# Block-masked attention with routed experts on one core: where the table scatters stand on GpSimd's queue

## The chip, the cores and the metric

The kernel runs on one core of a Trainium2 chip. A time is the device time of one execution in microseconds. The engines are TensorE (PE, with its weight loads as PEld), VectorE (DVE), ScalarE (ACT), GpSimd (POOL) and SyncE (SP, which issues DMAs). Each runs its own instructions in order and waits on semaphores for the others.

## The reference

Attention over 8 batches of 8 heads, 576 positions and 64 features, in which a position sees all blocks of 64 up to its own; then a layer of 8 experts of which each token uses one.

```python
mask = block_i >= block_j
scores = np.where(mask, scale * np.matmul(q, k.transpose(0, 1, 3, 2)), -1e9)
attn = np.exp(scores - np.max(scores, axis=-1, keepdims=True))
attn = attn / (np.sum(attn, axis=-1, keepdims=True) + 1e-09)
x = np.matmul(attn, v)               # then 4608 tokens of 512 features
expert_idx = np.argmax(logits, axis=1)
for e in range(E):                   # tokens grouped by expert
    mask = expert_idx == e
    h = np.maximum(x[mask] @ w1[e], 0.0)
    out[mask] = gate_w[mask, None] * (h @ w2[e])
```

## The kernel before, in words

The attention part (some 365 us) goes through 32 pairs of heads, four pairs to a batch. The expert part behind it takes the tokens in tiles of 128 that share an expert.

For a pair, `prep` turns q and k on TensorE (line 325); ScalarE and VectorE split them into a high and a low half (qh, ql, kh, kl, lines 342 and 344). `maxes` makes scores once to find each row's maximum (scores at line 360, maxima nmx on VectorE at 366); the maxima are turned and put beside q by a DMA (nmT, qa, lines 378 and 381). `scores` makes the scores again (line 421), ScalarE turns them into exponentials (pA and pT, line 428 and 430) and GpSimd adds these up over the key tiles into pS (`add`, lines 399, 400 and 402). `values` multiplies with v (line 456), and ScalarE copies the result out of PSUM as oe (line 462). `finish` turns oe and the sums back on TensorE, takes reciprocals (rin, line 531) and writes x into xrow. Scores live in four PSUM tiles (psm) that go round, so TensorE's next scores wait until ScalarE or VectorE has read the tile that it wants.

After a batch's fourth pair, `route` finds each token's expert and its place among that expert's tokens. It ends with five scatters (line 671): DMAs issued by GpSimd, each of which writes 128 token numbers of 4 bytes into places of `table` in DRAM. A scatter waits for nothing but an older DMA. At a batch's last scatter SyncE also issues one store of x (`store_piece`, line 575). Batch 5 (EB) is special: behind its scatters the first places of the table are read back (et, line 710), so that two tiles of tokens can be fetched early (line 716).

Each of these functions yields between its steps, and a string of letters per pair (`FIRST`, `STEADY`, `FINAL`) says which advances next: s for scores, v for values, m for maxes, p for prep, f for finish, l for loads, r for one step of the oldest unfinished route. That alone sets the order of instructions on every engine. STEADY has 11 letters r for pairs 5 to 26 (counted from 0); FINAL has a string for each of the last five.

Of the kernel before, what the change touches and what calls it, by code (L numbers as in the profile page):

```python
# [28 lines left out]
    "pfvvvvvpmvrvvrvpmrrssslmmsrsmrmmssprprsrvvsrvmfpfmfsrffm",  # L29
)  # L30
FINAL = (
    "rmmvrrvmvvvvrvvspvsrmpsrrrsrvfmvsvrrmrmfflsprrrfvvvrvmmrsfsffrrpvppsspvvppvmvssrrmrmvrvvmmrsmrsrmmsfrfsffssfprrrsmlvfprm",
    "srvmvpmmrvvrrvmrrrrvrrmppmmrrmvvrrrvvrrrrrmrrrrrrrlp",
    "slrvrrrrmrpsrprrsrsrspsrrrmmssrrrssrrrrrmssmmrmsrfrrfvvrvvrr",
    "rfvfsrrrmrrsmrfvfmrrrrsrrmsvmrvvrrvvrrsrrfrfrvfrrrsfvvfrsvvfvvrvrfrr",
# [13 lines left out]
def kernel(  # L49
# [522 lines left out]
    def store_piece():  # L572
        b, xrow, j = pieces.pop(0)
        r0 = b * S + 1 + j * P
        nc.sync.dma_start(xbuf[r0:r0 + P, :], xrow[:, j, :])
        if j == NJ - 2:
            nc.sync.dma_start(xbuf[r0 + P:r0 + P + 64, :], xrow[0:64, NJ - 1, :])
# [8 lines left out]
    def route(b, xrow, lgh, ssp):  # L586
# [80 lines left out]
            store(b, xrow, (NP - 1) * P, RW)  # L667
        yield
        if b < B - 1:
            for j in range(NJ):  # L670
                w = nc.gpsimd.indirect_dma_start(
                    out=table, out_offset=bass.IndirectOffsetOnAxis(ap=rowj[:, j:j + 1], axis=0),
                    in_=tokf[:, b, j:j + 1], in_offset=None, bounds_check=E * RE * P - 1, oob_is_err=False)
                for o in writes:
                    tc.declare_no_dep(w.ins, o.ins, reason="each place is written once")
                writes.append(w)
                if (b == B - 2 or j == NJ - 1) and pieces:
                    store_piece()
                yield
            if b == EB:  # L680
                early_g.append(early_rows())

    EB = B - 3
# [23 lines left out]
    def early_rows():  # L707
        et = rt.tile([P, EARLY], F32, name="et")
        none = rt.tile([P, EARLY], F32, name="enone")
        nc.sync.dma_start(et, table.rearrange("(p r) o -> p (r o)", p=P)[:, 0:EARLY])  # L710
        yield
        while pieces:
            store_piece()
        nc.gpsimd.tensor_copy(ei[:, 0], et)
        for u in range(EARLY):
            nc.gpsimd.indirect_dma_start(
                out=ex[u], out_offset=None, in_=xbuf[0:1 + (EB + 1) * S, :],
                in_offset=bass.IndirectOffsetOnAxis(ap=ei[:, 0, u:u + 1], axis=0))
            yield
        indices(nc.gpsimd, None, ei[:, 1], et, none)  # L720
# [63 lines left out]
    def post(n):  # L784

        b = n // NP
        xrow, rin, lgh, ssp = tiles(b)
        yield from finish(n, xrow, rin, lgh, ssp)
        if n % NP == NP - 1:
            slow.append(route(b, xrow, lgh, ssp))  # L790
        yield
# [400 lines left out]
    def chain():  # L1192
# [4 lines left out]
        for c in fg:  # L1197
            if c == "squares":
                break
            yield c  # L1200
        ch_sq.append(fg)
        rg = route(B - 1, xrow, lgh, ssp)
        for c in rg:
            if c == "counted":
# [106 lines left out]
    a, b = ea  # L1311
# [201 lines left out]
```

## Time and profile before

| | |
|---|---|
| median of 3 runs | 814.71 us (812.38 to 814.80) |
| profiled execution, its own time | 814.69 us |
| its span | 813.0 us |
| TensorE busy | 780.4 us (96%) |
| VectorE busy | 604.4 us (74%) |
| GpSimd busy | 436.4 us (54%) |
| ScalarE busy | 408.1 us (50%) |
| scatters of line 671 | 35, of 966 to 1157 ns (median 978) |

The span is the time from the first instruction to the last in the profiled execution; the execution's own time holds 1.7 us more. A busy share is a mean over stages with different limits. A timeline row gives the start (us from the span's start), the duration, the engine, the line, what is written and read, and in brackets the idle time ahead of it with what the profile thinks ended that. "issue" is a wait for which it found nothing.

### The profile page before, as it was taken

How to read it: one execution, taken by the hardware profiler on the slowest of the kernel's cores; microseconds unless marked ns; L12 is line 12 of the kernel's file. 1: busy time of each engine (PE TensorE's matmuls, PEld its weight loads, DVE VectorE, ACT ScalarE, POOL GpSimd, SP SyncE). 2: the span in 40 equal slices, each digit the busy share in tenths (PEclk: the TensorE clock that was granted, in tenths of full speed). 3: DMA queues.
4: the chain of work that ended last, by engine and by line, in shares of the span. 5: the costliest groups of instructions: out<-in, count | busy, mean ns of one | idle time of the engine just before them, and what ended most of it. 6: DMA issues, size and time to landing. Idle time of an engine off the chain costs nothing. (4 is left out here: it accounts for less than half of the span.)

```text
span 813.0 us, 23042 instructions
## 1 busy us (share of the span) xinstructions
PE 780.4 (96%) x7160; PEld 628.6 (77%) x7160; DVE 604.4 (74%) x1382; ACT 408.1 (50%) x831; POOL 436.4 (54%) x420
## 2 busy tenths in 40 slices
PE   8999999999989998889999999999999999999996
PEld 3688877787878776668778887788888888888885
DVE  6668777786868686659858777777887778877881
ACT  2566756575757564664745355553533332543222
POOL 7555767667666756772337278675661111561110
PEclk9999999999999999999999999999999999999999
DMA  4745364544444543163835347444441111111111
GB/s 104 167 104 138 82 163 99 152 104 122 104 126 100 139 100 100 29 241 118 293 129 179 106 157 225 160 158 158 144 146 54 54 55 42 40 49 54 54 36 39
DMA packets 141422, 93.96 MB, mean 116 GB/s; under 512 B 118925, under 2 KB 120541, under 8 KB 141260
## 3 DMA queue, kind: packets, MB, share of 16 engines
q1 hardware_dynamic: 133228, 69.74, 30.8%
q0 software_dynamic: 8032, 22.36, 8.4%
q8 instruction: 66, 1.08, 0.5%
q14 instruction: 96, 0.79, 0.3%
HBM read 72.71 MB, written 19.71 MB: 114 GB/s over the span
## 5 line engine op out<-in xcount | busy, mean ns | idle before, releaser
L1167 DVE STREAM_TRANSPOSE pt<-h 32x256 f32<-32x256 f32 x528 | 240.7, 456 | 31.2 <-ACT h L1141 14.0
L366 DVE TENSOR_REDUCE nmx<-psm 128x16 f32<-128x1024 f32 (+2 forms) x128 | 125.5, 985 | 22.0 <-PE psm L360 19.4
L912 POOL TENSOR_TENSOR ring_l<-raw,ring_h 128x1024 f32 (+1 forms) x49 | 116.2, 2400 | 37.5 <-ACT ring_h L907 23.8
L1181 POOL DMA_INDIRECT out_dram<-y,outi x36 | 37.2, 1034 | 177.5 <-ACTq L1061 118.1
L1114 PE MATMUL py<-ring_h,hh 128*128 x272 | 109.3, 402 | 0.8 <-ACT h L1141 0.8
L1114 PE MATMUL py<-ring_l,hh 128*128 x272 | 106.3, 391 | 0.0
L428 ACT ACTIVATE pT<-psm 128x640 f32<-128x640 f32 (+2 forms) x128 | 89.0, 702 | 27.2 <-PE psm L360 15.8
L402 POOL TENSOR_TENSOR pS<-pS,pT 128x640 f32<-128x640 f32 (+2 forms) x93 | 93.4, 1004 | 10.4 <-ACT pT L430 2.8
L1114 PE MATMUL py<-ring_h,hl 128*128 x272 | 88.8, 389 | 0.0
L1114 PE MATMUL ph<-ring_h,xh 128*128 x280 | 86.5, 390 | 1.7 <-ACT y L1180 1.1
L1114 PE MATMUL ph<-ring_l,xh 128*128 x280 | 86.4, 390 | 1.5 <-POOLq L1073 1.5
L456 PE MATMUL psm<-pT,vo 128*64 128x320 f32 (+2 forms) x640 | 76.1, 380 | 0.3 <-ACT pT L428 0.3
L1180 ACT ACTIVATE y<-py,xg 128x512 f32<-128x512 f32 x34 | 23.4, 688 | 103.2 <-PE py L1114 99.7
L1175 DVE TENSOR_TENSOR hl<-pt,hh 128x512 fp32r<-128x512 f32 x66 | 42.5, 686 | 42.6 <-ACT hh L1173 37.6
L421 PE MATMUL psm<-qh,kh 64*128 64x320 f32 (+4 forms) x384 | 66.9, 344 | 7.1 <-ACT pT L428 3.6
L907 ACT CAST ring_h<-raw 128x1024 f32 (+1 forms) x62 | 60.9, 1048 | 22.3 <-POOLq L1073 9.7
L1173 ACT CAST hh<-pt 128x512 fp32r<-128x512 f32 x66 | 35.5, 590 | 72.9 <-DVE pt L1167 72.5
L1114 PE MATMUL ph<-ring_h,xl 128*128 x280 | 69.2, 389 | 0.0
L456 PEld LDWEIGHTS psm<-pT,vo 128*64 128x64 f32 x640 | 43.2, 137 | 28.6 <-ACT pT L428 0.8
L1114 PEld LDWEIGHTS ph<-ring_h,xh 128*128 128x128 f32 x280 | 52.4, 188 | 13.2 <-ACT y L1180 1.5
L1114 PEld LDWEIGHTS ph<-ring_l,xh 128*128 128x128 f32 x280 | 52.5, 188 | 12.8 <-POOLq L1073 1.9
L1114 PEld LDWEIGHTS ph<-ring_h,xl 128*128 128x128 f32 x280 | 52.6, 188 | 10.9
(289 smaller groups left out, 1683.9 us busy)
## 6 DMA issues: line engine op xcount, KB each, us to landing
raw<-in_moe_w_dram SPq DMA_DIRECT2D x60, 512.0 KB
qn<-in_q_dram SPq DMA_DIRECT2D x64, 128.0 KB
kn<-in_k_dram SPq DMA_DIRECT2D x64, 128.0 KB
vo<-in_v_dram SPq DMA_DIRECT2D x64, 128.0 KB
xbuf<-xrow SPq DMA_DIRECT2D x28, 260.0 KB
raw<-in_moe_w_dram POOLq DMA_DIRECT2D x4, 512.0 KB
qa<-nmT SPq DMA_DIRECT2D x64, 2.5 KB
xbuf<-xrow SPq DMA_DIRECT2D x7, 130.0 KB
```

What stands on the lines that cost most here:

```text
L366: nc.vector.tensor_reduce(m[:, :, f:f + o // w], mt[:, :, 0:o].rearrange("p h (b c) -> p h b c", c=w), axis=AX.X, op=ALU.max, negate=True)
L402: nc.gpsimd.tensor_tensor(o, o, pT[:, :, off[t]:off[t] + w], op=ALU.add)
L421: nc.tensor.matmul(st[0:kw, hh, o:o + c1 - c0], kk[hd[hh], t * P:t * P + kw], qq[hd[hh], 64 + c0:64 + c1], start=(x == 0), stop=(x == len( ...
L428: nc.scalar.activation(pT[:, :, f:f + w] if c0 else pA, st[:, :, 0:w], AF.Exp, scale=scale)
L456: m = nc.tensor.matmul(ob[hh * D:(hh + 1) * D, b0:b0 + q1 - c0], rows(vo, ends_v, n, t)[:, hh, :], pTs[hh][0][:, f0:f0 + q1 - c0] if c0 el ...
L907: return (nc.scalar.copy if eng is nc.scalar else eng.tensor_copy)(piece(ring_h, to, c, half), raw[i][:, c * CW:(c + 1) * CW])
L912: return eng.tensor_tensor(piece(ring_l, to, c, half), raw[i][:, c * CW:(c + 1) * CW], piece(ring_h, to, c, half).bitcast(F32), op=ALU.sub ...
L1114: m = nc.tensor.matmul(out, ac, slots[g]["w", i](r, c * n + off), start=(u == 0 and c == 0), stop=(c == nk - 1 and u == len(turns) - 1))
L1167: nc.vector.transpose(pt[32 * j:32 * j + 32, :, 32 * i:32 * i + 32], h[32 * i:32 * i + 32, :, j, :])
L1173: nc.scalar.copy(sets["hh"][u], pt[:, 4 * u:4 * u + 4])
L1175: nc.vector.tensor_tensor(sets["hl"][u], pt[:, 4 * u:4 * u + 4], sets["hh"][u].bitcast(F32), op=ALU.subtract)
L1181: nc.gpsimd.indirect_dma_start(out=out, out_offset=bass.IndirectOffsetOnAxis(ap=to, axis=0), in_=y, in_offset=None, bounds_check=NT - 1, o ...
```

## The change

The route of batches 0 to 4 gets three empty steps ahead of its first scatter and eight between the third and the fourth. Five letters r are taken out of the string of pair 27 (pairs are counted from 0), so that batch 5's scatters come in the pair behind. Everything that is not a scatter, or the store beside a batch's last scatter, keeps its place.

```diff
 FINAL = (
-    "rmmvrrvmvvvvrvvspvsrmpsrrrsrvfmvsvrrmrmfflsprrrfvvvrvmmrsfsffrrpvppsspvvppvmvssrrmrmvrvvmmrsmrsrmmsfrfsffssfprrrsmlvfprm",
+    "rmmvrrvmvvvvrvvspvsrmpsrrrsrvfmvsvrrmrmfflsprrfvvvvmmsfsffpvppsspvvppvmvssrrmrmvrvvmmrsmrsrmmsfrfsffssfprrrsmlvfprm",
...
         if b < B - 1:
+            for _ in range(3 if b < EB else 0):
+                yield
             for j in range(NJ):
+                if j == 3 and b < EB:
+                    for _ in range(8):
+                        yield
                 w = nc.gpsimd.indirect_dma_start(
                     out=table, out_offset=bass.IndirectOffsetOnAxis(ap=rowj[:, j:j + 1], axis=0),
                     in_=tokf[:, b, j:j + 1], in_offset=None, bounds_check=E * RE * P - 1, oob_is_err=False)
```

GpSimd's instructions at the scatters of batch 0, in the kernel before; lines 399 to 402 are the additions of a pair, and the two numbers of pT tell one pair from the next:

```order
L671 DMA table<-tokf,rowj 36864x1 x3
L399 TENSOR_TENSOR pS<-pA,pT_211 128x2x128
L400 TENSOR_TENSOR pS<-pT_211 128x2x320
L671 DMA table<-tokf,rowj 36864x1 x2
L402 TENSOR_TENSOR pS<-pS,pT_211 128x2x320
L402 TENSOR_TENSOR pS<-pS,pT_211 128x2x192
L402 TENSOR_TENSOR pS<-pS,pT_211 128x2x64
L399 TENSOR_TENSOR pS<-pA,pT_212 128x2x128
L400 TENSOR_TENSOR pS<-pT_212 128x2x320
L402 TENSOR_TENSOR pS<-pS,pT_212 128x2x320
```

The same place now; a scatter is line 676 here:

```order
L399 TENSOR_TENSOR pS<-pA,pT_211 128x2x128
L400 TENSOR_TENSOR pS<-pT_211 128x2x320
L676 DMA table<-tokf,rowj 36864x1 x2
L402 TENSOR_TENSOR pS<-pS,pT_211 128x2x320
L676 DMA table<-tokf,rowj 36864x1
L402 TENSOR_TENSOR pS<-pS,pT_211 128x2x192
L402 TENSOR_TENSOR pS<-pS,pT_211 128x2x64
L399 TENSOR_TENSOR pS<-pA,pT_212 128x2x128
L400 TENSOR_TENSOR pS<-pT_212 128x2x320
L676 DMA table<-tokf,rowj 36864x1 x2
L402 TENSOR_TENSOR pS<-pS,pT_212 128x2x320
```

The three scatters ahead of a pair's additions are gone from there: two stand behind its second addition, one behind its third, and the last two behind the second addition of the next pair. Batches 1 to 4 read alike.

GpSimd at the scatters of batch 5, before:

```order
L399 TENSOR_TENSOR pS<-pA,pT_212 128x2x128
L400 TENSOR_TENSOR pS<-pT_212 128x2x320
L671 DMA table<-tokf,rowj 36864x1 x3
L402 TENSOR_TENSOR pS<-pS,pT_212 128x2x320
L671 DMA table<-tokf,rowj 36864x1 x2
L402 TENSOR_TENSOR pS<-pS,pT_212 128x2x192
L402 TENSOR_TENSOR pS<-pS,pT_212 128x2x64
L399 TENSOR_TENSOR pS<-pA,pT_211 128x2x128
```

And now:

```order
L399 TENSOR_TENSOR pS<-pA,pT_212 128x2x128
L400 TENSOR_TENSOR pS<-pT_212 128x2x320
L402 TENSOR_TENSOR pS<-pS,pT_212 128x2x320
L402 TENSOR_TENSOR pS<-pS,pT_212 128x2x192
L402 TENSOR_TENSOR pS<-pS,pT_212 128x2x64
L676 DMA table<-tokf,rowj 36864x1 x5
L399 TENSOR_TENSOR pS<-pA,pT_211 128x2x128
```

All five moved behind the pair's last addition and stand in one row ahead of the next pair's first.

On SyncE one store of x per batch (batches 0 to 4) moves from the pair of the first scatters, where two stood ahead of that pair's qa, to the next pair, where two stand now.

## Rows read from the trace of the kernel before

**Rows 1.** The page's busy time (us, share of the span, instructions).

```profile
PE 780.4 (96%) x7160; PEld 628.6 (77%) x7160; DVE 604.4 (74%) x1382; ACT 408.1 (50%) x831; POOL 436.4 (54%) x420
```

**Rows 2.** Table of stretches: length, busy per engine (instructions), TensorE clock, DMA.

```profile
98.89:109.98 11.09, 10.27 (x161) 8.13 (x157) 7.63 (x17) 5.81 (x12) 8.04 (x8) 1.00 0.45 121
109.98:119.48 9.50, 9.50 (x161) 8.05 (x158) 7.25 (x17) 5.92 (x12) 7.59 (x8) 1.00 0.86 213
139.61:150.91 11.30, 10.03 (x160) 7.99 (x156) 7.05 (x16) 5.09 (x11) 8.22 (x8) 1.00 0.42 112
150.91:161.23 10.32, 9.87 (x162) 7.98 (x158) 7.71 (x17) 6.61 (x14) 7.30 (x8) 1.00 0.79 200
171.73:181.39 9.66, 9.66 (x160) 8.02 (x156) 8.12 (x24) 6.76 (x17) 7.12 (x9) 1.00 0.38 88
181.39:192.68 11.29, 10.06 (x161) 8.00 (x158) 7.05 (x16) 5.11 (x11) 8.23 (x8) 1.00 0.42 113
192.68:202.98 10.30, 9.87 (x161) 7.98 (x157) 7.71 (x17) 6.61 (x14) 7.25 (x8) 1.00 0.60 146
...
223.15:235.19 12.04, 10.11 (x161) 7.97 (x157) 5.97 (x16) 5.76 (x12) 8.97 (x9) 1.00 0.40 108
235.19:245.63 10.44, 9.82 (x157) 8.03 (x158) 8.69 (x18) 6.08 (x13) 6.55 (x7) 1.00 0.59 144
265.79:277.03 11.24, 10.04 (x160) 8.00 (x156) 7.05 (x16) 5.12 (x11) 8.22 (x8) 1.00 0.43 116
277.03:287.33 10.30, 9.87 (x161) 7.98 (x158) 7.71 (x17) 6.61 (x14) 7.29 (x8) 1.00 0.61 149
```

**Rows 3.** Timeline: start, duration, instruction [idle before]; GpSimd, 181 to 193.

```profile
181.58 1.09 POOL L671 DMA_INDIRECT table<-tokf,rowj  x1 [0.27 <-issue]
...
189.38 0.99 POOL L671 DMA_INDIRECT table<-tokf,rowj  x1 [0.16 <-ACT nmT L378]
190.67 0.97 POOL L671 DMA_INDIRECT table<-tokf,rowj  x1 [0.30 <-issue]
```

**Rows 4.** Timeline of ScalarE in the same stretch.

```profile
182.94 0.60 ACT L428 ACTIVATE pA<-psm 128x512 f32<-128x512 f32 x1 [1.00 <-PE psm L421]
...
192.52 0.37 ACT L462 COPY oe<-psm 128x256 f32<-128x256 f32 x1 [2.83 <-remote]
```

**Rows 5.** Timelines of ScalarE, GpSimd, VectorE in the stretch behind.

```profile
193.80 0.60 ACT L428 ACTIVATE pA<-psm 128x512 f32<-128x512 f32 x1
...
201.10 0.37 ACT L462 COPY oe<-psm 128x256 f32<-128x256 f32 x1 [1.06 <-PE psm L456]
...
197.59 1.56 POOL L400 TENSOR_TENSOR pS<-pT 128x640 f32<-128x640 f32 x1
...
199.71 0.17 DVE L531 TENSOR_SCALAR rin<-psm 128x8 f32<-128x8 f32 x1 [0.80 <-PE psm L325]
```

**Rows 6.** TensorE's waits in the stretch from 181.39: waited for, us, times, longest.

```profile
PE psm L421 <- ACT pT L428: 0.5, 1, 0.5
PE psm L325 <- DVE nmx L366: 0.4, 1, 0.4
```

**Rows 7.** Timeline of TensorE near batch 5's scatters.

```profile
311.27 0.50 PE L360 MATMUL psm<-kh,qh 64*128 64x448 f32 x4 [1.72 <-issue]
```

**Rows 8.** Table of stretches: 4 us behind that stall.

```profile
312.00:316.00 4.00, 4.00 (x53) 3.63 (x44) 3.11 (x6) 1.02 (x2) 2.46 (x3) 0.57 0.30 88
```

**Rows 9.** Timelines of VectorE and TensorE behind the scatters of 231 to 233.

```profile
233.52 0.17 DVE L531 TENSOR_SCALAR rin<-psm 128x8 f32<-128x8 f32 x1 [2.50 <-PE psm L456]
...
236.32 0.39 PE L421 MATMUL psm<-qh,kh 64*128 64x256 f32 x2 [0.62 <-DVE nmx L366]
```

**Rows 10.** Timeline of SyncE's queue, 313 to 320.

```profile
314.18 0.34 SPq L710 DMA_DIRECT2D et<-table  x1
319.13 1.41 SPq L381 DMA_DIRECT2D qa<-nmT  x2
```

**Rows 11.** GpSimd's waits over the whole span.

```profile
POOL pS L399 <- ACT pT L428: 67.9, 28, 7.2
```

## The prediction

> **What bounds the kernel now.** I read the page's busy table first, then a table of stretches, then the instructions of single stretches on GpSimd, ScalarE, VectorE and TensorE. TensorE is busy for 96% of the span [rows 1], so 32.6 us of idle time is all that any reordering can win, apart from time in which TensorE's clock is lowered. The change touches only the attention part, which ends near 365 us, so I cut that part at the one TensorE instruction that comes once per pair (the 64x448 scores of line 360). A stretch from one such start to the next is one pair of heads [rows 2]. All of them hold nearly the same TensorE work. The quickest without scatters, 171.73 to 181.39, has TensorE busy for all of its 9.66 us; I take 9.66 as the price of a pair that waits for nothing. Every fourth stretch is the one with a batch's five table scatters. Five of these are shown: 11.09, 11.30, 11.29, 12.04 and 11.24 us. The stretches right behind them take 9.50, 10.32, 10.30, 10.44 and 10.30 us [rows 2].
>
> What happens there is seen in the stretch from 181.39. Three scatters follow each other at its start, the first at 181.58 and each some 1.0 us long with 0.3 between, while TensorE makes scores; the fourth and fifth start at 189.38 and 190.67 [rows 3], while TensorE multiplies probabilities with values. No row says that anybody waits for a scatter. But ScalarE's copies start late. Its first exponential (pA) starts at 182.94 after a wait of 1.00, and the copy oe at 192.52 after 2.83 [rows 4]. In the stretch behind, without scatters, pA starts with no wait shown and oe waits 1.06 [rows 5]. TensorE then waits itself, 0.5 us for pT and 0.4 us for VectorE's nmx [rows 6], because the PSUM banks come free late; its idle time in this stretch is 11.29 - 10.06 = 1.23 us [rows 2]. So a scatter makes TensorE's finished work known late to ScalarE and VectorE. That is an inference from the times, and it is the heart of the forecast. The lateness seems to begin near a scatter's end: the fifth ends at 191.64 [rows 3] and oe starts 0.88 us behind that.
>
> The Trainium skill has a rule that speaks against this reading. "SBUF — State Buffer", section "SBUF: two separate sides", says that only VectorE and GpSimd can hold each other up, by an exclusive lock on a port pair, and that TensorE and ScalarE never wait on anyone. By it the place of a scatter is worth nothing to ScalarE, the change would move no time, and the run would stay at 814.7. The trace disagrees as far as ScalarE's late starts go (1.00 and 2.83 us), so the sum goes by the rows; the rule stands behind the first rival.
>
> **The change part by part.** It removes and adds no instruction that computes or moves data. By the order, TensorE, ScalarE and VectorE keep theirs; GpSimd and SyncE get theirs moved.
>
> *Batches 0 to 4, GpSimd.* Before, three scatters stand ahead of a pair's first addition and two behind its second. Now two stand in the place of the last two, one behind the next addition, and the last two behind the second addition of the pair that follows. So of five scatters one is left near the start of a stretch, where scores are made, and four lie where values are made. The prices come from rows 2:
> - A scatter in the score part: the five stretches exceed 9.66 by 1.43, 1.64, 1.63, 2.38 and 1.58, together 8.66 us for 15 such scatters, 0.577 us each.
> - A scatter in the value part: its cost, if any, falls on the stretch behind. Those exceed 9.66 by -0.16, 0.66, 0.64, 0.78 and 0.64, together 2.56 us for 10 scatters, 0.256 us each.
>
> Before, the five batches pay 8.66 + 2.56 = 11.22 us. After, 5 x 0.577 + 20 x 0.256 = 2.89 + 5.12 = 8.01. Gain 3.2 us.
>
> These prices can be wrong both ways. One scatter alone near a stretch's start could miss every signal and cost nothing, or cost 0.79 as in the worst stretch (2.38 / 3). Two in the value part could cost nothing (-0.16) or 0.78 (0.39 each). All low gives 0 - 1.6 = -1.6, a gain of 12.8; all high gives 3.95 + 7.8 = 11.75, a loss of 0.5. I take the means, since three of the five stretches lie within 0.06 us of each other in both places.
>
> One thing speaks for the new place being no dearer than the old. In the stretch free of scatters GpSimd ends its second addition at 197.59 + 1.56 = 199.15 and VectorE starts rin at 199.71 [rows 5]. A scatter in that place would start near 199.3, so rin's signal comes before that scatter's end. If lateness begins near the end, rin escapes. What is late there then is oe, as now.
>
> *Batch 5, GpSimd.* Its five scatters move from between the additions of one pair to a single row of five behind them, so ahead of the next pair's first addition. Today they let TensorE idle for 1.72 us before 311.27 [rows 7], and after that stall the granted clock falls: 0.57 in the mean from 312 to 316 [rows 8], between the two levels of 2.4 and 1.2 GHz, which loses 4.00 x 0.43 = 1.72 us. Together 3.44. In the new place they lie beside scores; five at 0.577 cost 2.9. Gain 0.55 us. From below: if five in a row cost no more than the three of the first stretch (1.43), the gain is 2.0; if they bring the same idle time and the same clock twice over, 3.4 us are lost.
>
> *SyncE.* One store of the rows of x moves from the scatters' stretch to the next in each of five batches. The store then stands ahead of that stretch's load of qa, as it does today in the scatters' stretch, where TensorE's waits are for pT and nmx and not for a load [rows 6]. DMA engines are busy for 0.59 to 0.86 of the stretch behind [rows 2], so they have room; the other loads there serve the pair after the next two. I take 0; if qa came late, the nearest measured wait of TensorE is 0.5 us [rows 6], so 2.5 us for five batches.
>
> *The wait behind batch 5.* SyncE's load of et waits for all five scatters, and it starts at 314.18 [rows 10]. Queued behind it is the load of qa at 319.13 [rows 10], which the next scores need. The last scatter is set back past the two short additions, together no longer than the 1.56 us of the large one [rows 5], which leaves over 3 us of that gap. I take 0; if the gap were gone because the scores come earlier, the delay is at most those 1.6 us.
>
> *GpSimd's additions* behind a moved scatter come up to 2.6 us later (two scatters of 0.99 and 0.97 [rows 3] and their gaps), but GpSimd waits for pT ahead of a pair's first addition, 67.9 us in 28 pairs or 2.4 us each [rows 11]: that covers them within 0.2 us, which I take as 0.
>
> **Sum.** 3.2 + 0.55 = 3.75 us. The profiled execution took 814.69 us (span 813.0), 0.02 us below the median shown, so no shift is needed: 814.69 - 3.75 = 810.9.
>
> **The rivals.**
>
> *No change: the stall only moves.* As many scatters run as before, each holds signals up for about as long, and TensorE meets some signal everywhere. For it: the cost per scatter in the value part rests on five stretches, one of which shows none, and the new pair of value places lies 1.3 us earlier in the pair than the old. Then only batch 5's part is left, 0 to 0.55 us: 814.4. The Trainium skill's rule on ports, told above, would end here too. Against it: the 9.66 us stretch shows that pairs far from scatters lose nothing.
>
> *Slower: rin is caught.* In the new place VectorE's rin lies just ahead of the lateness. In the batch at 223.15 it was caught: rin waited 2.50 and started at 233.52, so the maxima behind it came late and TensorE waited 0.62 us at 236.32 [rows 9]. If both new value places of a batch do this, ten stretches lose 0.62: 6.2 us on top, so 810.9 + 6.2 = 817.1. Some of these waits could join with the third scatter's into one of 1.7 us, behind which the clock falls as at 311.27; one such fall in each batch adds 5 x 1.72 = 8.6, 825.7. It decides from the point at which rin's wait passes about 1.9 us (2.50 less 0.62). Against it: the margin worked out from rows 5: rin would start at 199.71, 0.6 us ahead of the end of a scatter of 0.99 from 199.3.
>
> *Larger gain: value places are free.* TensorE's work on values is long and depends on nothing that a scatter makes late, and the first batch shows 9.50 behind its scatters. If the four cost nothing, the gain is 11.22 - 2.89 + 0.55 = 8.9: 805.8. Against it: four of five stretches behind cost 0.64 or more.
>
> **How the numbers follow.** Forecast (the prices above, 808 to 812.3): 0.46. No change: 0.28. Slower: 0.12. Larger gain: 0.14. What a measurement of this kernel can tell from no change is about 0.3%, 2.4 us, so the bound for faster is 812.3 and for slower 817.2. Faster: 0.46 + 0.14 = 0.60. Same: 0.28 and 0.04 of the slower case, whose first size (817.1) lies at the bound. Slower: the other 0.08. The range leaves out the far half of the larger gain and the slower case: 806.6 to 815.2. The likeliest one's own range is 808 to 812.3.
>
> **What would show it.** In the profile after, the stretches that now take 11.09 to 12.04 should be near 9.8; those behind them near 10.7, with one late pA or pT; the next near 10.8, with oe late. At 312 to 316 the granted clock should stay at 1.00. The forecast is wrong if oe and pA are late in the same number of places as now, if rin shows waits of 2 us, or if the granted clock falls in more than one place of the attention part.

## The result, and the profile after

| | before | after |
|---|---|---|
| median | 813.69 us (812.27 to 814.80, 6 runs) | 823.62 us (820.39 to 828.56, 6 runs) |
| profiled execution, its span | 814.69, 813.0 us | 823.60, 821.9 us |
| mean granted clock | 0.997 | 0.985 |

The ratio is 1.0117, 95% interval 1.0093 to 1.0140: 1.2% slower, where 0.5% faster was forecast. TensorE's busy time rose, which no added work explains. The page's busy line (us, share, instructions), to be held against [rows 1]:

```profile
PE 785.8 (96%) x7160; PEld 634.6 (77%) x7160; DVE 610.8 (74%) x1382; ACT 408.8 (50%) x831; POOL 437.3 (53%) x420
```

The stretches of batches 0 and 2, in the columns of [rows 2]:

```profile
98.84:108.37 9.53, 9.53 (x161) 8.05 (x158) 7.06 (x16) 5.81 (x12) 5.14 (x5) 1.00 0.42 107
108.37:117.93 9.56, 9.56 (x160) 8.02 (x156) 7.70 (x17) 5.38 (x13) 8.49 (x9) 1.00 0.89 238
...
192.19:202.05 9.86, 9.72 (x160) 8.02 (x156) 7.78 (x17) 5.57 (x13) 8.69 (x9) 1.00 0.71 180
202.05:216.10 14.05, 11.79 (x166) 9.40 (x162) 10.07 (x25) 8.53 (x20) 7.34 (x10) 0.88 0.42 104
```

and the third stretch of batch 2 before, in the same view:

```profile
202.98:213.48 10.50, 10.25 (x167) 8.37 (x163) 8.45 (x25) 8.08 (x19) 5.58 (x7) 1.00 0.46 116
```

The first two stretches of a batch, where the prediction had its prices, became short. The third, for which it gave "near 10.8, with oe late", became long. A batch has four stretches; all of them, cut at the same TensorE instruction (us):

| stretch | before | after | sum of the change |
|---|---|---|---|
| first, batches 0 to 4 | 11.09, 11.30, 11.29, 12.04, 11.24 | 9.53, 9.52, 9.52, 9.51, 9.52 | -9.4 |
| second, batches 0 to 4 | 9.50, 10.32, 10.30, 10.44, 10.30 | 9.56, 9.86, 9.86, 9.85, 9.88 | -1.9 |
| third, batches 0 to 3 | 10.51, 10.50, 10.50, 10.50 | 14.15, 11.91, 14.05, 15.22 | +13.3 |
| the two behind these, up to 329.99 before and 338.37 after | 23.94, 18.72 | 26.23, 22.74 | +6.3 |

With 0.01 for the fourth stretches, -0.05 ahead of all and 0.5 behind them this is the span's 8.9 us. The last row holds batch 4's third stretch, with the same three waits as in the others (0.75, 0.40 and 1.12 us, ahead of 293.01, 294.38 and 296.02), and batch 5's scatters.

That the stall left the first two is seen on ScalarE. Batch 2's first pA starts 0.07 us behind the end of its last matmul (183.45 + 0.28 = 183.73); before it started 0.50 us behind it (182.16 + 0.28 = 182.44, [rows 4]). ScalarE's timeline after:

```profile
183.80 0.60 ACT L428 ACTIVATE pA<-psm 128x512 f32<-128x512 f32 x1 [0.58 <-PE psm L421]
```

What happens in the third stretch begins on GpSimd, one stretch earlier. Its timeline after (columns as in [rows 3]):

```profile
186.57 0.74 POOL L399 TENSOR_TENSOR pS<-pA,pT 128x256 f32<-128x256 f32 x1 [4.00 <-ACT pT L428]
...
193.11 0.99 POOL L676 DMA_INDIRECT table<-tokf,rowj  x1 [0.17 <-issue]
194.12 1.58 POOL L402 TENSOR_TENSOR pS<-pS,pT 128x384 f32<-128x384 f32 x2
196.14 0.74 POOL L399 TENSOR_TENSOR pS<-pA,pT 128x256 f32<-128x256 f32 x1 [0.44 <-ACT pT L428]
...
199.84 0.97 POOL L676 DMA_INDIRECT table<-tokf,rowj  x1 [0.30 <-issue]
200.82 3.20 POOL L402 TENSOR_TENSOR pS<-pS,pT 128x640 f32<-128x640 f32 x3
203.98 0.26 POOL L597 TENSOR_TENSOR lg<-lg,mx 128x40 f32<-128x40 f32 x1
...
206.70 1.53 POOL L400 TENSOR_TENSOR pS<-pT 128x640 f32<-128x640 f32 x1
```

Line 597 is a step of the next batch's route (lg less mx), queued behind the second pair's additions. Its input mx ends at 202.21 + 0.20 = 202.41; it starts 1.57 us later, because the additions end late. In the kernel before GpSimd waited 2.06 us for pT ahead of that pair and 1.02 us for mx ahead of line 597:

```profile
196.90 0.73 POOL L399 TENSOR_TENSOR pS<-pA,pT 128x256 f32<-128x256 f32 x1 [2.06 <-ACT pT L428]
...
203.41 0.25 POOL L597 TENSOR_TENSOR lg<-lg,mx 128x40 f32<-128x40 f32 x1 [1.02 <-DVE mx L595]
```

VectorE's timeline after shows who waits for it:

```profile
202.21 0.20 DVE L595 TENSOR_REDUCE mx<-lg 128x5 f32<-128x40 f32 x1
202.52 0.82 DVE L344 TENSOR_TENSOR ql<-psm,qh 128x640 fp32r<-128x640 f32 x1
204.27 0.20 DVE L600 SCALAR_TENSOR_TENSOR t<-lg,erev 128x40 f32<-128x40 f32 x1 [0.92 <-POOL lg L597]
204.39 1.22 DVE L366 TENSOR_REDUCE nmx<-psm 128x16 f32<-128x1024 f32 x1
...
207.01 1.27 DVE L604 TENSOR_TENSOR hot<-t,mx 128x40 bf16<-128x40 f32 x1
```

Line 600 waits 0.92 us, where it waited for nothing before, and the maxima of line 366 stand behind it, which free PSUM tiles. Then comes a second effect: line 604, at 0.19 us in the kernel before (206.71), takes 1.27. It ends at 208.28, 0.05 us behind the end of GpSimd's addition (206.70 + 1.53 = 208.23). It had been due before that addition started; late, it falls beside it and is held until it ends. TensorE waits for both:

```profile
205.66 0.30 PE L360 MATMUL psm<-kh,qh 64*128 64x64 f32 x2 [0.75 <-DVE nmx L366]
...
207.02 0.47 PE L325 MATMUL psm<-ident,kn 64*128 64x64 f32 x8 [0.41 <-DVE nmx L366]
...
208.66 0.18 PE L615 MATMUL psm<-hot,triS 128*128 128x40 bf16 x1 [1.11 <-DVE hot L606]
```

And the clock falls behind these waits (table of stretches, the clock is the third number from the right):

```profile
208.00:210.00 2.00, 1.34 (x42) 1.21 (x41) 1.55 (x7) 1.50 (x5) 1.20 (x2) 1.00 0.00 0
210.00:211.00 1.00, 1.00 (x18) 1.00 (x18) 0.22 (x1) 0.31 (x1) 0.66 (x2) 0.56 0.00 0
211.00:212.00 1.00, 1.00 (x20) 1.00 (x20) 0.00 (x0) 0.66 (x3) 0.00 (x0) 0.50 0.00 0
212.00:213.00 1.00, 1.00 (x13) 0.70 (x13) 0.80 (x4) 0.74 (x3) 0.88 (x1) 0.50 0.01 2
213.00:214.00 1.00, 1.00 (x12) 0.73 (x12) 1.00 (x5) 0.00 (x0) 0.58 (x2) 0.73 0.01 3
```

The sum for this stretch: TensorE idle for 14.05 - 11.79 = 2.26 us against 0.25 before, 2.0 more; the low clock loses 14.05 x 0.12 = 1.7. Together 3.7, and the stretch is 3.55 longer.

Batch 5's five scatters in one row, TensorE's timeline after:

```profile
322.04 0.30 PE L360 MATMUL psm<-kh,qh 64*128 64x64 f32 x2 [4.01 <-issue]
```

It stands until the fifth of them ends (321.12 + 0.97 = 322.09), where it stood 1.72 us before [rows 7].

### The profile page after: what moved, and what is told of

It reads as the page before. It is cut to its first block, busy times and chain, and to the rows that moved or that the text cites. A ratio compares the mean times of both kernels' runs of the same rounds, so it can differ in the third digit from the quotient of the medians.

```text
span 821.9 us, 23041 instructions
## 1 busy us (share of the span) xinstructions
PE 785.8 (96%) x7160; PEld 634.6 (77%) x7160; DVE 610.8 (74%) x1382; ACT 408.8 (50%) x831; POOL 437.3 (53%) x420
## 5 line engine op out<-in xcount | busy, mean ns | idle before, releaser
L366 DVE TENSOR_REDUCE nmx<-psm 128x16 f32<-128x1024 f32 (+2 forms) x128 | 125.5, 986 | 17.7 <-PE psm L360 10.5
```

Source lines behind the costliest of these rows:

```text
L366: nc.vector.tensor_reduce(m[:, :, f:f + o // w], mt[:, :, 0:o].rearrange("p h (b c) -> p h b c", c=w), axis=AX.X, op=ALU.max, negate=True)
```

## The experiments

The theory after this reading: the moved scatters make GpSimd's additions late, line 597 with them, and through lines 600, 366 and 604 TensorE; the clock adds to it. In the expectations this is theory 1. The rivals: the scatters' new places hold TensorE's signals as the old ones did; batch 5's row (theory 2); the clock falls because the stretches are denser (theory 3); the moved stores (theory 4); any scatter in the second stretch (theory 5); line 604's length alone.

Kernels under one letter ran on the same chip together with the kernel before: A and C on chip 1, B on 7, D on 11, E on 15. Before took 796.5 to 796.7 us with A, C and E, and 813.9 to 814.4 with B and D, as in the first comparison. What differs is told below. The stretches are those of the profiled execution, whose time can lie some us from the median: a_again's took 808.61 us, its other four 813.55 to 815.88.

| | kernel | us | ratio to before | third stretches |
|---|---|---|---|---|
| A | a_final_old | 811.33 | 1.0196 (1.0175 to 1.0216) | 12.06 to 14.09 |
| A | b_final_only | 797.11 | 1.0006 (0.9997 to 1.0016) | 10.5 |
| A | c_lg_vector | 813.00 | 1.0223 (1.0191 to 1.0255) | 11.69 to 15.17 |
| A | e_no_scatter | 803.07 | 1.0077 (1.0060 to 1.0093) | 10.50 to 11.13 |
| B | k_lead0_gap8 | 817.77 | 1.0043 (1.0024 to 1.0062) | 10.5 |
| B | k_lead0_gap11 | 831.47 | 1.0222 (1.0189 to 1.0254) | 12.07 to 15.55 |
| B | g_gap0 | 809.69 | 0.9946 (0.9929 to 0.9963) | 10.5 |
| B | k_fill | 828.84 | 1.0147 (1.0087 to 1.0206) | 15.3 to 15.5 |
| C | a_again | 815.28 | 1.0238 (1.0220 to 1.0255) | 12.06 to 12.57 |
| C | k_hot_scalar | 830.14 | 1.0423 (1.0406 to 1.0441) | 15.05 to 16.02 |
| C | k_both | 831.22 | 1.0423 (1.0395 to 1.0451) | 15.05 to 15.84 |
| C | g_one_late | 809.69 | 1.0183 (1.0123 to 1.0243) | 11.59 to 12.57 |
| D | idle_late | 837.56 | 1.0295 (1.0261 to 1.0329) | 13.45 to 14.87 |
| D | idle_covered | 818.54 | 1.0068 (1.0044 to 1.0092) | 11.07 to 12.56 |
| D | g_gap0_b | 808.48 | 0.9930 (0.9901 to 0.9959) | 10.5 to 11.06 |
| D | after_b | 825.75 | 1.0143 (1.0098 to 1.0187) | 14.13 to 15.30 |
| E | idle_26 | 814.48 | 1.0208 (1.0182 to 1.0234) | 12.57 to 15.46 |
| E | g_gap0_final | 811.89 | 1.0199 (1.0172 to 1.0225) | 14.03 to 15.49 |

**The two halves of the change.** a_final_old is the changed kernel with the old string of pair 27, b_final_only the kernel before with the new one.

```diff
 a_final_old, against after; b_final_only, against before, the other way round
-    "rmmvrrvmvvvvrvvspvsrmpsrrrsrvfmvsvrrmrmfflsprrfvvvvmmsfsffpvpp...
+    "rmmvrrvmvvvvrvvspvsrmpsrrrsrvfmvsvrrmrmfflsprrrfvvvrvmmrsfsffrrpvpp...
```

> The changed kernel with the old string of pair 27, so that only the scatters of batches 0 to 4 are moved and batch 5's stand where they stood before. Theory 1 (the route's subtraction on GpSimd, line 597, comes late behind the moved additions; VectorE waits for it ahead of its maxima, then its compare of line 604 meets an addition on GpSimd; TensorE waits and its clock falls): the third stretches of the batches stay at 11.9 to 15.2 us, and the time is 4 to 5 us above before, near 818.5. Theory 2 (the five scatters of batch 5 in a row are the cost): the time falls below before, near 811.

> The kernel before with the new string of pair 27 alone, so that only batch 5's five scatters are moved. Theory 1: it costs the smaller part, 2 to 3 us, since one old stall of 1.72 us with its clock loss goes and one longer stall of 4.0 us comes: near 816. Theory 2: the whole loss of about 10 us is here: near 823.

On this chip the loss is all in batches 0 to 4: 2.0% with them alone, 0.06% with the string alone. The surprise lies elsewhere. In b_final_only the scatters of batches 0 to 4 keep the old order, and yet their stretches take 9.51 to 9.52 us, not 11.1 to 12.0. On this chip the scatters hold nothing up (nor on E, where idle_26 has the old order too and 9.51 to 9.52 us), so there was no stall to win back, and only the loss is left. GpSimd's timeline of b_final_only:

```profile
180.34 0.97 POOL L671 DMA_INDIRECT table<-tokf,rowj  x1 [0.30 <-issue]
181.41 0.73 POOL L399 TENSOR_TENSOR pS<-pA,pT 128x256 f32<-128x256 f32 x1
...
190.97 0.74 POOL L399 TENSOR_TENSOR pS<-pA,pT 128x256 f32<-128x256 f32 x1 [1.66 <-ACT pT L428]
...
196.97 0.25 POOL L597 TENSOR_TENSOR lg<-lg,mx 128x40 f32<-128x40 f32 x1 [0.51 <-DVE mx L595]
```

The old order puts three scatters into the time in which GpSimd has no pT yet: the first addition follows the third scatter with no wait shown. In the changed order that wait stands empty at 4.00 us (186.57 above).

**Line 597 off GpSimd.**

```diff
-        eng.tensor_tensor(lg, lg, bc(mx.unsqueeze(2), P, NJ, E), op=ALU.subtract)
+        nc.vector.tensor_tensor(lg, lg, bc(mx.unsqueeze(2), P, NJ, E), op=ALU.subtract)
```

> The changed kernel with the subtraction of line 597 on VectorE instead of GpSimd for batches 0 to 6; all scatters stay moved. Theory 1: VectorE no longer waits for GpSimd, TensorE's waits for the maxima and for the compare go, the third stretches come down to about 10.5 us, and the time falls by up to 17 us from 823.6, to 807 to 812 (the part of batch 5 stays). If VectorE and GpSimd hold each other up on a shared port, the subtraction itself may take up to 1.5 us instead of 0.2 where it meets an addition, and the time lies at the upper end. Theory 3 (TensorE's clock falls because the stretches are denser): no change, 823.

No gain. VectorE no longer waits for GpSimd, but line 597, with two SBUF inputs, now meets an addition there itself and takes 0.82 us, and line 604 takes 1.31:

```profile
203.80 0.82 DVE L597 TENSOR_TENSOR lg<-lg,mx 128x40 f32<-128x40 f32 x1
...
207.71 1.31 DVE L604 TENSOR_TENSOR hot<-t,mx 128x40 bf16<-128x40 f32 x1
```

So the run doesn't tell the theory from its rivals: it traded one delay for another.

**No scatters.** Leaves out the scatters of batches 0 to 4, so their tokens are missing from the table.

```diff
                 if j == 3 and b < EB:
                     for _ in range(8):
                         yield
+                if b < EB:
+                    if j == NJ - 1 and pieces:
+                        store_piece()
+                    yield
+                    continue
```

> The changed kernel without the scatters of batches 0 to 4 (their tokens are then missing from the table, so most of the output rows are not computed); everything else is in its place, the empty steps too. Theory 1: GpSimd is never behind, the third stretches take about 10.5 us or less and the other stretches 9.5 to 9.9; about 806 to 807. Theory 3 (density): the clock falls in the third stretches all the same and the time stays near 823. Theory 4 (the store of x that moved on SyncE delays a load): the third or second stretches stay long too, since the store still moves.

The third stretches go back to 10.50 to 11.13 at a granted clock of 1.00 and line 604 to 0.19 in the median; the attention part ends as early as with b_final_only (the last cut at 313.11 against 312.76). The scatters make the loss; the empty steps, the moved stores and the density of the stretches don't. The 6 us by which the whole is still slower arise behind the attention part, where the table lacks tokens; their cause is open.

**Which scatters.** All three are the kernel before or the changed one with other numbers of empty steps (lead ahead of the first scatter, gap between third and fourth), and the old string of pair 27.

```diff
 k_lead0_gap8: lead 0, gap 8; k_lead0_gap11: lead 0, gap 11; g_gap0: lead 3, gap 0
-            for _ in range(3 if b < EB else 0):
+            for _ in range(LEAD if b < EB else 0):
...
-                    for _ in range(8):
+                    for _ in range(GAP):
```

> The kernel before with eight empty steps between the third and the fourth scatter of batches 0 to 4 and nothing else (no empty steps ahead, old string of pair 27). On GpSimd the first three stay ahead of a pair's first addition, where it waits for exponentials anyway; the last two come to the same place of the next pair. Theory 1 (what costs is that GpSimd has no free time between its additions, so it is still behind when the next route wants its subtraction): no scatter stands between additions, GpSimd is on time, the third stretches take 10.5 us and the time equals before within 0.3%. Theory 5 (scatters in the second stretch are bad wherever they stand there): slower by 10 us or more, like the kernel with only batches 0 to 4 moved.

> As the one with eight empty steps, but with eleven: the last two scatters then stand behind the second addition of the next pair, as in the changed kernel, and the first three where they stood before. Theory 1: these two alone set the additions and the subtraction of line 597 back by about 2.6 us, the third stretches take 12 to 15 us, and the time is 10 to 15 us above before. Rival (the two plus one scatters in the first pair are needed for the loss): within 3 us of before.

> The changed kernel with the old string of pair 27 and without the eight empty steps: all five scatters lie among the additions of the first pair, none in the second. Theory 1 in its stricter form (GpSimd's work of two pairs and five scatters has to end before the next route starts, and no free time lies between): GpSimd is about as late at line 597 as in the changed kernel, and the loss stays at 8 us or more. Rival (only the last two, in the second pair, matter): the time equals before within 0.5%.

With gap 8 the last two stand ahead of the next pair's first addition, where GpSimd waits for pT anyway: line 597 is on time, the third stretches 10.5. The whole is still 0.4% slower than before, where at most 0.3% was expected: four of its second stretches take 10.76 to 10.79 us, and one first stretch 13.00 at a clock of 0.87. With gap 11 they stand behind that pair's second addition, as in the change, and the first three where they always were: third stretches up to 15.55 and 2.2% lost, against 1.2 to 1.4% for the changed kernel on such chips, as the stall of the first three stays (first stretches of 11.04 to 11.28). GpSimd's timeline of k_lead0_gap11:

```profile
205.25 0.97 POOL L676 DMA_INDIRECT table<-tokf,rowj  x1 [0.30 <-issue]
206.22 3.20 POOL L402 TENSOR_TENSOR pS<-pS,pT 128x640 f32<-128x640 f32 x3
209.38 0.26 POOL L597 TENSOR_TENSOR lg<-lg,mx 128x40 f32<-128x40 f32 x1
...
212.14 1.53 POOL L400 TENSOR_TENSOR pS<-pT 128x640 f32<-128x640 f32 x1
```

and VectorE's: line 600 waits, line 604 starts beside line 400 and ends 0.06 us behind it (213.73 and 213.67).

```profile
209.67 0.20 DVE L600 SCALAR_TENSOR_TENSOR t<-lg,erev 128x40 f32<-128x40 f32 x1 [0.77 <-POOL lg L597]
...
212.42 1.31 DVE L604 TENSOR_TENSOR hot<-t,mx 128x40 bf16<-128x40 f32 x1
```

So the last two alone, in the new place, bring the loss. g_gap0 has none of them there (four in the first pair, the fifth ahead of the next one's first addition) and is faster than both kernels on this chip, against the theory's stricter form; on E below it is not.

**Keeping TensorE busy in its wait.** a_final_old with six spare matmuls of 128x512 ahead of line 615 in batches 0 to 6.

```diff
+        if b < B - 1:
+            for _ in range(6):
+                nc.tensor.matmul(rb[:, 1, 0:512], onesb, bc(onesb.unsqueeze(1), P, 4, P), start=True, stop=True)
         nc.tensor.matmul(rk, triS, ohb, start=True, stop=False)
```

> The changed kernel with the old string of pair 27, and six matmuls more (128x512 in bfloat16, whose result nobody reads) on TensorE ahead of the route's first matmul (line 615) in batches 0 to 6, where TensorE waits for VectorE's compare. They are put into time that is idle. Theory 1 with the clock: the waits stay, but TensorE is kept at work and its granted clock does not fall in the third stretches, so they get shorter by up to 1.7 us each, some 8 us in all, to 803 to 806. Rival (the clock falls for the earlier waits, or for something else than idle time): no gain, or a loss of 1 us per batch.

A miss. Their PSUM tile comes out of the same four, so they waited themselves, and the clock fell (0.50 from 172 to 174). It says nothing on the theory.

```profile
170.96 2.63 PE L617 MATMUL psm<-onesb 128*128 128x512 bf16 x6 [0.99 <-DVE nmx L366]
```

**Line 604 with one SBUF tensor.** k_hot_scalar is a_final_old with line 604 as five operations; k_both does the same to line 597 as well, on VectorE. a_again is a_final_old beside them.

```diff
-        nc.vector.tensor_tensor(ohb, t1, bc(mx.unsqueeze(2), P, NJ, E), op=ALU.is_equal)
+        for j in range(NJ):
+            nc.vector.tensor_scalar(ohb[:, j, :], t1[:, j, :], mx[:, j:j + 1], None, op0=ALU.is_equal)
```

> The scatters of batches 0 to 4 moved as in the change, the string of pair 27 as before; the reference for the three runs beside it. Third stretches of 12 to 15 us, line 600 waiting some 5 us in all for line 597, line 604 near 1.1 us in the median, the time 1.5 to 2% above the kernel before; no theory says otherwise.

> Line 604 as five tensor_scalar operations with one SBUF tensor each instead of one operation with two. Theory that line 604 is slow because it reads two SBUF operands while a GpSimd addition runs: the five together take about 0.5 us and never 1.3, TensorE's wait for hot falls from about 1.1 to about 0.5 us, the third stretches fall by 1 to 3 us each and the time by some 4 to 8 us, though line 600 still waits for line 597. Rival, that it is only late (its start, not its length, is what the TensorE waits for): the third stretches stay at 12 to 15 us and the time within 2 us of the reference.

> Line 597 on VectorE instead of GpSimd, and it and line 604 as five tensor_scalar operations each, with one SBUF tensor. If the whole loss is line 597 queued behind late additions together with the slow line 604, both causes are gone here: third stretches 10.5 to 11.3 us, no granted clock below 0.9 in the attention part, the time at or below that of the kernel before (0 to 8 us less). If the later scatters hold back something else as well, the third stretches stay above 12 and the time above the kernel before.

Both expectations fell: the operation was held in this form too. VectorE's timeline of k_hot_scalar:

```profile
212.46 0.20 DVE L600 SCALAR_TENSOR_TENSOR t<-lg,erev 128x40 f32<-128x40 f32 x1 [1.47 <-POOL lg L597]
...
215.20 0.90 DVE L605 TENSOR_SCALAR hot<-t,mx 128x8 bf16<-128x8 f32 x1
...
216.01 0.62 DVE L605 TENSOR_SCALAR hot<-t,mx 128x8 bf16<-128x8 f32 x4
```

The first of the five ends at 216.10, when the addition on GpSimd does (214.53 + 1.54 = 216.07), and the other four come on top. Hot is later than in a_again, TensorE's waits for it grow from 3.2 to 12.4 us in all, and every third stretch takes 15 to 16 us instead of 12.1 to 12.6 (in a_again's fastest execution). The third stretch of batch 2 in k_hot_scalar:

```profile
209.89:225.60 15.71, 12.95 (x167) 10.29 (x164) 10.12 (x29) 8.18 (x19) 7.68 (x10) 0.78 0.38 94
```

TensorE is idle half a microsecond longer than in a_again (2.76 against 12.56 - 10.30 = 2.26), and the clock is 0.78 instead of 1.00. That the half microsecond brought the clock down is not shown (next experiment), nor what the loss would be with line 604 free.

**One scatter late instead of two.** a_final_old with the gap between the fourth and the fifth.

```diff
-                if j == 3 and b < EB:
+                if j == 4 and b < EB:
```

> Four scatters in the first pair and only the fifth behind the next pair's second addition, with the eight empty steps ahead of it. GpSimd's later additions come 1.3 us late instead of 2.6. Theory that the lateness has to pass the slack ahead of line 597 (it came 1.6 us late in the changed kernel): line 597 comes within 0.4 us of its input, line 604 at 0.19, third stretches about 10.5 to 11, the time at or below the kernel before. Rival, that any scatter inside the second pair's additions brings the loss: third stretches above 12 us, the time 1% or more above it.

The rival came nearer: the loss is 1.8%, though two of the four third stretches stay below 12 us. It doesn't show that 1.3 us are enough, since the four scatters among the first pair's additions had used up the wait for pT, and the next pair's first addition starts with none shown (194.41). In the stretch of 12.57 us line 600 waits 0.97 and line 604 takes 1.44 beside the addition. TensorE is idle in it for as long as in the changed kernel (12.57 - 10.31 = 2.26 us), but the clock stays at 1.00:

```profile
199.20:211.77 12.57, 10.31 (x166) 8.24 (x162) 9.79 (x25) 8.20 (x19) 7.17 (x10) 1.00 0.38 97
```

So a third stretch near 12.5 is the waits alone, one of 14 to 15.5 the waits and the clock. Both occur in one execution of one kernel: batches 2 and 3 of a_final_old, with the same idle time (2.27 and 2.26 us):

```profile
200.38:212.96 12.58, 10.31 (x167) 8.25 (x164) 9.28 (x25) 8.20 (x19) 7.69 (x10) 1.00 0.38 97
...
241.67:255.76 14.09, 11.83 (x168) 9.64 (x164) 9.37 (x25) 8.20 (x19) 7.66 (x10) 0.88 0.37 95
```

The waits thus come with the order of the kernel; the fall of the clock behind them comes in some stretches and not in others.

**Lateness without scatters.** The kernel before, with its own scatter order, and spare memsets on GpSimd in batches 0 to 4: behind the next pair's second addition (idle_late, 9 empty STEPS), or ahead of its first (idle_covered, 5); idle_26 is idle_late with nine memsets.

```diff
+            if b < EB:
+                for _ in range(STEPS):
+                    yield
+                for _ in range(2):
+                    for _ in range(7):
+                        nc.gpsimd.memset(dumt, 0.0)
+                    yield
```

> The kernel before with no scatter moved, and in batches 0 to 4 fourteen memsets of a spare tile on GpSimd (about 2.6 us by the rate of the other memsets) where the change puts a batch's last two scatters, behind the second addition of the next pair. Theory that the loss is GpSimd's additions, and line 597 behind them, being late, whatever makes them late: line 600 waits for line 597, line 604 is held to near 1.2 us, third stretches of 12 to 15 us, the time 1.3 to 2.3% above the kernel before. Rival, that it takes scatters there (their descriptors, their DMAs, or late signals): third stretches stay at 10.5 and the time within 0.3% of the kernel before.

> The same fourteen memsets, ahead of that pair's first addition instead of behind its second, where GpSimd waits for pT (2.06 us there in the kernel before). Theory that only lateness at line 597 counts: the wait covers them but for 0.5 us or so, third stretches 10.5 to 11.2 us, the time within 0.5% of the kernel before. Rival, that 2.6 us of GpSimd's time in that pair costs by itself, wherever it stands: third stretches above 12 us as with idle_late.

> As idle_late, with nine memsets instead of fourteen: they took 0.286 us each there (4.00 for 14), so nine are 2.6 us, as long as the two scatters that the change puts in this place. If lateness of GpSimd is the whole mechanism, line 597 comes some 1 to 1.6 us behind its input as in the changed kernel, line 604 is held to near 1.2 us and the third stretches take 12 to 15 us; the time lies between those of idle_covered (1.007) and idle_late (1.030), about 1.5 to 2.3% above the kernel before. If scatters add something of their own, the third stretches stay below 11.5 and the time below 1.010.

So lateness on GpSimd is enough, whatever makes it. The fourteen memsets took 4.00 us, not 2.6. Behind the second addition they make line 597 late and cost 3.0%; the same 4.00 us one step earlier, where GpSimd waits for pT, cost 0.7%. That is a little more than the 0.5% expected, since 4.00 us are more than the wait of 2.06: line 600 still waits 3.8 us in all, against 13.3 in idle_late. GpSimd's timeline of idle_late:

```profile
206.51 4.00 POOL L685 MEMSET dumt<- 128x160 f32 x14
210.47 3.19 POOL L402 TENSOR_TENSOR pS<-pS,pT 128x640 f32<-128x640 f32 x3
213.62 0.25 POOL L597 TENSOR_TENSOR lg<-lg,mx 128x40 f32<-128x40 f32 x1
```

VectorE's: the wait is 2.41 us, and line 604, by now behind the addition's end, takes its 0.19.

```profile
213.91 0.20 DVE L600 SCALAR_TENSOR_TENSOR t<-lg,erev 128x40 f32<-128x40 f32 x1 [2.41 <-POOL lg L597]
...
216.66 0.19 DVE L604 TENSOR_TENSOR hot<-t,mx 128x40 bf16<-128x40 f32 x1
```

The stretch takes 14.87 all the same, and over the attention part TensorE waits 11.8 us for maxima ahead of line 360 and 0.9 for hot. So line 604 is no needed part of the loss. With nine memsets (idle_26), about as long as two scatters, line 600's waits are 7.7 us over six batches (7.7 in a_final_old and a_again, 5.1 in the changed kernel of the first comparison) and the third stretches 12.57 to 15.46: 2.1%, as a_final_old and a_again cost on such a chip (2.0 and 2.4%). No scatter had been moved.

**The faster order, on both kinds of chip.** g_gap0_b is g_gap0 again, after_b the changed kernel beside it; g_gap0_final is g_gap0 with the new string of pair 27.

> Three empty steps ahead of the scatters and none between them, string of pair 27 as before: the version that took 0.9946 of the time before where the table scatters held signals up. If its gain is that stall gone, then on a chip where the kernel before shows no such stall it gains nothing (0.997 to 1.003, third stretches 10.5), and on one where it does it gains 0.4 to 0.7% again.

> The changed kernel beside the other three. Where the kernel before shows the stall of the scatters, 1.0 to 1.4% above it; where it doesn't, there is nothing to win back and the whole loss of the third stretches shows: 1.7 to 2.5% above it. Its time exceeds that of g_gap0_b by 1.5 to 2.3% on either chip.

> The version with three empty steps and no gap, now with the change's new string of pair 27, so that batch 5's five scatters stand in one row. The kernel before with that string alone showed no difference, but on a chip where scatters held nothing up. In the profile after, TensorE stood for 4.01 us until the fifth of them ended, where it stood 1.72 in the kernel before. If that wait is the price of the row of five, this kernel takes 2 to 4 us more than g_gap0 did (0.993 to 0.995 of the time before), so 0.996 to 1.000, where the scatter stall shows; if the string is free, 0.993 to 0.995 again. Without a scatter stall, 0.998 to 1.002.

On D g_gap0_b gains 0.7% again and the changed kernel loses 1.4%. On E, where the old order's scatters cost nothing, g_gap0_final loses 2.0%, against an expectation of 0.998 to 1.002. The string is not the cause, by b_final_only, and the long third stretches all lie ahead of pair 27; what is left is the order of the scatters. GpSimd's timeline of g_gap0_final:

```profile
190.32 0.73 POOL L399 TENSOR_TENSOR pS<-pA,pT 128x256 f32<-128x256 f32 x1 [3.97 <-ACT pT L428]
...
200.93 0.99 POOL L676 DMA_INDIRECT table<-tokf,rowj  x1 [0.24 <-issue]
201.95 0.74 POOL L399 TENSOR_TENSOR pS<-pA,pT 128x256 f32<-128x256 f32 x1
```

The wait of 3.97 us ahead of the first pair is left empty, all five scatters come behind it, and the next pair's additions start with no wait left. Line 600 then waits 6.2 us over six batches. On D the same order gets that time back, since TensorE is held up in the second stretch (10.34 to 10.89 us there, 9.50 to 9.54 on E), and mx comes later too: in g_gap0_b line 600 waits 1.0 us in all. So the order of g_gap0 beats the kernel before only where scatters hold TensorE up. No order that I ran is faster on both kinds of chip.

## Why the prediction was wrong

The step that failed is the last term: that "*GpSimd's additions* behind a moved scatter come up to 2.6 us later" and that the wait for pT "covers them within 0.2 us, which I take as 0". The size was about right: the last two scatters and their gaps take 2.4 us (198.39 to 200.82). The cover was wrong twice:
- The wait for pT lies ahead of a pair's first addition, and the scatters were put behind the second. The next such wait comes one pair later, and line 597 stands before it. The prediction asked when the next pair's additions start, not what else stands in GpSimd's queue; in the changed kernel's order line 597 stands behind that pair's two remaining additions, just below the last row that was shown.
- 2.4 us was a mean over 28 pairs [rows 11]. In the pair in question the wait was 2.06 us before and is 0.44 after. A third scatter now stands among the first pair's additions, which end 0.86 us later (195.70 against 194.84), and pT comes 0.76 us earlier, as the stall is gone.

The place that decides, 1.02 us ahead of line 597, was in the trace of before. Its price could have been bounded from there: 2.6 - 1.02 = 1.6 us of VectorE ahead of the maxima, five times, and the clock behind it by [rows 8]: 5 x (1.6 + 1.72) = 16.6 us, 3.3 a batch. The loss measured in the third stretches of four batches is 13.3, also 3.3 each. That the two agree is in part luck: line 600 waited 0.92 us and not 1.6, and line 604's delay is not in the sum.

The rest, by its steps:
- *Batches 0 to 4, the stall.* The direction was right and the size too small. First stretches were to be near 9.8 and are 9.5; second near 10.7 and are 9.9. The two gained 11.2 us where 3.2 was forecast, so scatters in the value part were nearly free, as the rival of a larger gain had it (the low end was 12.8). The base was too high as well: a stretch that waits for nothing takes 9.5 us, not 9.66. The inference behind the stall, that TensorE's finished work becomes known late, is borne out by pA (0.50 us behind its last matmul before, 0.07 after, above). In the rival's sum, too, the lateness of the additions was missing.
- *Batch 5.* Taken as a gain of 0.55. In the trace after TensorE stands 4.01 us, and the granted clock from 322 to 326 is 0.60, losing 4.00 x 0.40 = 1.6; before it was 1.72 and 1.72. That is a loss of 2.2, inside the bound of 3.4. From 312 to 316 the clock did stay at 1.00, as was forecast, but only because the stall now comes at 318. after_b shows the stall again (3.94 us). On A the string costs nothing; alone on a chip that stalls it wasn't run.
- *No change.* This did not happen; but on A, C and E, where the old places hold nothing up, there was indeed nothing to win.
- *Slower: rin is caught.* The sign was right, the mechanism wrong. Rin waits 0.80 at 198.78, as in [rows 5]. Of what would show the forecast wrong, the fall of the clock in more than one place came true, behind waits that the rival didn't have.
- *SyncE, and the wait behind batch 5.* TensorE's waits for qa come to 0.2 us in the whole attention part of the changed kernel; both terms of 0 stand.

Not settled: why the same scatters hold up TensorE's signals on some chips and not on others. Nor does a run free line 597 alone: c_lg_vector and k_both took it off GpSimd, and VectorE was held elsewhere. That the lateness reaches TensorE through lines 597, 600 and 366 is read from the waits in the traces, and idle_late, where line 604 keeps its 0.19 us, is the clearest of them.

## What to carry to other kernels

When a DMA issue is moved down an engine's queue, follow every instruction behind it to its consumer, and from there the consumer's own queue, until a wait is found that lies between the moved piece and that consumer; a wait ahead of the piece, or a mean over many, covers nothing. Time in which an engine has no input yet is free to that engine, and moving DMA issues out of it spends slack elsewhere. It need not be the best place for the others: ahead of the first addition the scatters cost nothing on A, and on the chips of B and D a stretch took 11.0 us or more instead of 9.5. A gain won against a stall should be tried where the stall doesn't show, since an order can be faster on one chip and slower on the next.

## What the runs showed of the hardware

- Two kinds of chip: with the same scatters in the same places a scatter stretch takes 11.09 to 12.04 us in the first comparison and 9.51 to 9.52 on chips 1 and 15, and the whole kernel 814 (also on chips 7 and 11) and 796.5.
- A VectorE operation of 128x40 with two SBUF inputs that starts beside a GpSimd addition is held until that addition ends: 0.19 becomes 1.27, 1.31 and 1.44 us, ending 0.05 to 0.06 behind it. The Trainium skill's "SBUF — State Buffer", section "SBUF: two separate sides", tells of this lock between the two engines, and the trace agrees. Here an operation with one SBUF tensor and a column of scalars was held as well (0.90, k_hot_scalar), while VectorE's reductions out of PSUM kept their 1.22 beside additions.
- TensorE's idle pieces of 0.75, 0.41 and 1.11 us ahead of 208.66 in the changed kernel were followed by a granted clock of 0.50 to 0.73 from 210 to 214; pieces of 0.58, 0.40 and 1.28 in g_one_late were followed by 1.00. In a_final_old nearly the same pieces went both ways: 1.10, 0.40 and 0.77 ahead of 207.00 were followed by 1.00, and 1.09, 0.39 and 0.78 ahead of 248.28 by 0.50 from 249.8 to 251.8. Five executions of a_again had a mean clock from 0.984 (815.88 us) to 0.997 (808.61). What tips it was not found.
